# A gated mix of long convolution and multi-query attention on one core: x block 0 in two DMAs, the last x block by token chunks, the bound added to the first keys in place, and 88 instead of 92 score pairs on VectorE

## The chip, the core and the metric

The kernel runs on one core of a Trainium2 chip. The metric is the time of one execution on the device in microseconds (us). A profile of one execution belongs to it: the span is the time from the first to the last instruction in that profile. PE is TensorE, DVE is VectorE, ACT is ScalarE, POOL is GpSimd and SP is SyncE, which issues most DMAs.

## The reference: what is computed

S is 2048 tokens, D is 640 channels, there are 32 heads of 20 channels, and all heads share one key and one value of 20 channels. All inputs are bf16. Cut to what matters (left out: y is the causal convolution of kv with ssm_k along the tokens, by FFT):

```python
def _A_ref(q, k, v, shift_k, ssm_k, ssm_D):
    k_pad = jnp.pad(k, ((0, 0), (ks - 1, 0), (0, 0)))
    for t in range(ks):
        k_shift = k_shift + k_pad[:, t:t + S, :] * shift_k[:, ks - 1 - t][None, None, :]
    kv = k_shift * v
    ...
    y = y + kv * ssm_D[None, None, :]
    return q * y

def _B_ref(x, wq, wk, wv, wo):
    q = (x @ wq).reshape(B, S, H, Dh).transpose(0, 2, 1, 3)
    k = x @ wk
    v = x @ wv
    scores = jnp.einsum("bhqd,bkd->bhqk", q, k) * (Dh ** -0.5)
    p = _softmax(scores, axis=-1)
    o = jnp.einsum("bhqk,bkd->bhqd", p, v)
    return o.transpose(0, 2, 1, 3).reshape(B, S, H * Dh) @ wo

x = A_q
g = _sigmoid((x * gate_w).sum(-1, keepdims=True))
return g * _A_ref(x, A_k, A_v, A_shift_k, A_ssm_k, A_ssm_D) + (1 - g) * _B_ref(x, B_wq, B_wk, B_wv, B_wo)
```

## The kernel before

**A graph and a planner.** The kernel doesn't issue instructions as it goes. The methods of the class `Kernel` add operations (`Op`) to a graph: engine, function, keys read and written, an estimated cost and a priority. `Scheduler.run` (L204) then plays the program through once at build time with these costs, engine by engine, and picks for each engine the ready operation with the lowest priority number. The result is one fixed order for each engine, which `emit` (L544) writes out with the semaphore waits. On the chip every engine runs its order strictly; where the plan was off, an engine waits, and all that stands behind it in its order waits too. Where PE would be idle, the planner puts in filler matmuls: against zeros into an unused bank before attention starts (L1704), and against zeros into the accumulator (L1699) later. Matmul operations belong to groups that take one of 8 PSUM banks from a list and are evacuated by DVE or ACT.

**The work of attention.** Queries come in 4 blocks of 512 tokens; a head group is 4 heads on 4 x 32 rows of PE. So there are 32 (block, group) steps, named by G; a step has 16 key blocks j of 128 keys, and in each 4 score tiles (one per head r) of 128 keys x 512 queries. The last step (LASTG = 31) is split by queries into three stages (`STAGES`). `stream` (L1144) lines up all tiles in order and takes out those that go to DVE: for step G and each j in `DVE_J[G]` two of the four heads form a pair that DVE exponentiates by a polynomial (`DEXP`, L1231: two score matmuls, two L1257 out of PSUM, then L1260, L1261, L1263). It does this only where G < LASTG. The other tiles go to ACT in units of 3 and 2 by turns: `QK` (L1197, matmuls L1190) writes a unit's scores to PSUM banks 0 to 2 (ETA) or 3 to 4 (ETB), `EXP` (L1225, L1227) exponentiates them, and `PV` (L1273, L1268) multiplies the result with the values into a bank that gathers the step's output. The units of QK, EXP and PV are the main line; everything else is placed around it.

**Softmax without a maximum pass.** Each score gets a bound subtracted by way of the matmul itself: row 20 of each head's 32 query rows holds an estimate of the query's length (`cr`, from the squares of the queries: L1110, matmul L1118, L1124), and row 20 of the keys holds a factor from the largest key length (`mcol`, L1071). The row of the queries is written by a small DMA on SP (L1127, "qT<-cr"). So the scores of a group need its query projection (L1095), the square, the sum over a head's channels, `cr` and that DMA; and all scores need `mcol`.

**The prologue**, before the first exp:
- `loads` (L833): SP issues x block 0 (512 tokens x 640), the weights of the first query group, x blocks 1 to 3, then, when block 3 has landed, the rest of wq. ACT issues wk, wv and the gate's weights.
- `tables` (L892): the cosine and sine tables for the convolution, made by DVE (L905, L908) and ACT (L910).
- `weights`, `weights2`: POOL puts the weights into padded tiles; `wq_pad` is set to zero first (L869 for group 0, L991 for the rest), then filled (L984 and L995).
- `xT` (L999): PE transposes x by 128x128 blocks (L1008), ACT or DVE copies each bank of them to SBUF (L721, L720). Blocks 0 to 2 go in groups of two 128-channel slices, block 3 slice by slice.
- `kproj` (L1019): for each x block, L1035 makes keys, values and gate for each of its 4 token chunks (41 columns, "kvn"); ACT squares the keys (L1043), DVE sums (L1054) and takes the maximum (L1057), PE spreads it to all partitions (L1060), and three small DVE operations make `mcol` (L1064, L1068, L1071). The transposed keys come from L1027 per x block; the evacuation adds `mcol` per partition: the first 128 keys by ACT (L1081), all others by DVE (L1079).
- `qproj` (L1087): group 0 before the attention, then groups 1 and 2, 3 and 4, 5 and 6, 7 in its course (bank 7 alone), then the later query blocks (`qproj_next`).

**Around the attention** run the shifted keys of the convolution (`kshift`, L1467: DMA transposes and loads of v on SP, `kdiag` on DVE, L1494 on PE), the rest of the tables (`tables2`, L919), the convolution by matmuls with the tables (L1551, L1617; products on POOL, L1584) and the output projection (L1647). `norm` (L1332) divides a finished step. For the last step, `tail_o` (L1380) and `tail` (L1406) do so with short operations: transposes and a reciprocal on DVE (L1389, L1393, L1394, L1397), a last product (L1403) added to partial sums made ahead (`part`, L1364: L1373 and L1376), and L1458 for the last rows.

## Time and profile before

| | |
|---|---|
| runs of the kernel before | 872.35 us median of 3 (872.23 to 873.17) |
| the profiled execution | 872.47 us; its span 870.7 us |
| granted clock of TensorE | 0.999 |
| PE busy | 846.3 us (97%), 8157 matmuls |
| ACT busy | 856.9 us (98%), 769 instructions |
| DVE busy | 699.7 us (80%) |
| POOL busy | 380.4 us (44%) |
| L1227, ETA of 128x1536 | 373 times, 1628 ns mean |
| L1227, ETB of 128x1024 (and one of 128x512) | 373 times, 1205 ns mean |
| L1260, L1261, L1263 on DVE, 128x1024 | 92 times each, 1397, 1384 and 1446 ns mean |
| L1257 on DVE, 128x512 out of PSUM | 184 times, 687 ns mean |
| filler matmuls of L1699 | 944 |

A line of the profile's page or of its timeline names engine, line of the source, operation and what is written from what ("ETA<-ps"), with the count after an x. In a timeline the first number is the start in us from the span's start, the second the time in us that the instructions of the line cover; in brackets stands the idle time before and what ended it. In the chain of waits each piece is followed back from the last instruction to what released it. "SPq" is SP issuing a DMA; "issue" is time without a cause that the profile shows. A busy share is an average over the whole span: it doesn't tell which engine sets the end.

### The profile page before, as it was taken

Reading aid. Unit: us, or ns where it says so; the run is one execution under the profiler, and the core shown is the slowest. Engines: PE = TensorE matmul, PEld = TensorE weight load, DVE = VectorE, ACT = ScalarE, POOL = GpSimd, SP = SyncE. Lnnn points to the kernel's source line nnn. Section 1 sums busy time; section 2 is a strip of 40 time slices with the busy share of each in tenths; the row PEclk is TensorE's granted clock in tenths of the full one; section 3 lists DMA queues with packets and bytes.
Section 4 is the critical chain, followed back from the end, with each engine's and each line's share of the span. In section 5 each row is a group of like instructions: output and inputs, shape, how many; then the busy total and the mean of one; then the engine's idle time right before and its main releaser. Section 6 shows DMA issues by size and latency. Waiting matters only on the chain.

```text
span 870.7 us, 18888 instructions
## 1 busy us (share of the span) xinstructions
PE 846.3 (97%) x8157; PEld 352.7 (41%) x8177; DVE 699.7 (80%) x905; ACT 856.9 (98%) x769; POOL 380.4 (44%) x351
## 2 busy tenths in 40 slices
PE   8999999999999999999999999999999999999998
PEld 5334434443444344444334344444343344243344
DVE  8568884489899887988888888887889879888835
ACT  6999999999999999999999999999999999999997
POOL 4573005767434255635345745456761345710000
PEclk9999999999999999999999999999999999999999
DMA  6900020002000001000001120000100000040210
GB/s 196 209 15 8 22 44 14 14 14 43 20 21 15 16 12 44 20 21 14 20 8 32 33 58 14 20 11 17 45 20 20 14 11 4 14 112 29 66 67 33
DMA packets 49714, 30.72 MB, mean 35 GB/s; under 512 B 32477, under 2 KB 45662, under 8 KB 49630
## 3 DMA queue, kind: packets, MB, share of 16 engines
q1 hardware_dynamic: 49054, 29.29, 12.6%
q8 instruction: 64, 1.05, 0.5%
q10 hardware_dynamic: 576, 0.22, 0.1%
q14 instruction: 20, 0.16, 0.1%
HBM read 17.85 MB, written 6.02 MB: 27 GB/s over the span
## 4 chain that ended last, share of the span: by engine, by line
ACT 93%; PE 5%; DMA 1%; DVE 0%; SPq 0%; issue 0%
ACT ETA L1227 55%; ACT ETB L1227 38%; PE ps L1190 1%; DMA xn<-in_A_q_dram 1%; PE ps L1373 1%; PE ps L1095 1%; PE ps L1268 1%; PE ps L1494 1%; PE ps L1403 0%; PE ps L1008 0%; SPq L687 0%; PE ps L1035 0%; PE ps L1027 0%; PE ps L1118 0%; DVE outsb L1458 0%
## 5 line engine op out<-in xcount | busy, mean ns | idle before, releaser
L1227 ACT ACTIVATE ETA<-ps 128x1536 bf16<-128x1536 f32 x373 | 607.1, 1628 | 0.6 <-PE ps L1190 0.5
L1227 ACT ACTIVATE ETB<-ps 128x1024 bf16<-128x1024 f32 (+1 forms) x373 | 449.4, 1205 | 1.3 <-PE ps L1190 1.3
L1190 PE MATMUL ps<-qT,kT 32*128 32x512 bf16 (+2 forms) x2176 | 301.0, 372 | 14.5 <-ACT ETA L1227 8.0
L1584 POOL TENSOR_TENSOR Pp<-X,K 128x512 f32<-128x512 bf16 x120 | 164.0, 1383 | 146.5 <-DVE K L1572 48.9
L1257 DVE TENSOR_SCALAR dW<-ps 128x512 f32<-128x512 f32 x184 | 126.3, 687 | 65.9 <-PE ps L1190 64.4
L1190 PEld LDWEIGHTS ps<-qT,kT 32*128 32x128 bf16 x2176 | 76.5, 91 | 247.4 <-ACT ETB L1227 128.1
L1268 PE MATMUL ps<-ETA,vaug 128*32 128x512 bf16 (+2 forms) x1196 | 153.9, 371 | 0.0
L1268 PE MATMUL ps<-ETB,vaug 128*32 128x512 bf16 (+2 forms) x796 | 148.5, 371 | 0.0
L1263 DVE SCALAR_TENSOR_TENSOR ETd<-dX,dW 128x1024 int16<-128x1024 f32 x92 | 133.1, 1446 | 3.2 <-PE ps L1268 3.1
L1260 DVE SCALAR_TENSOR_TENSOR dX<-dW 128x1024 f32<-128x1024 uint16 x92 | 128.5, 1397 | 1.0
L1261 DVE SCALAR_TENSOR_TENSOR dX<-dX,dW 128x1024 f32<-128x1024 f32 x92 | 127.3, 1384 | 0.4
L1584 POOL TENSOR_TENSOR AB<-Pp 128x256 bf16<-128x256 f32 x80 | 66.1, 826 | 68.3 <-DVE dX L1260 24.6
L1617 PE MATMUL ps<-AB,Tcs 128*128 128x256 bf16 x600 | 89.4, 275 | 0.0
L1551 PE MATMUL ps<-ssm_kT,Tcs 128*128 128x256 bf16 x600 | 89.0, 275 | 0.0
L1551 PE MATMUL ps<-kv,Tcs 128*128 128x256 bf16 x600 | 87.4, 275 | 0.1
L1348 POOL TENSOR_TENSOR oTn<-acc,rbc 128x512 bf16<-128x512 f32 x24 | 39.9, 1661 | 88.5 <-DMA rbc<-scr_d 27.7
L1699 PE MATMUL ps<-Tcs,zeros 128*32 128x512 bf16 x944 | 77.9, 385 | 0.7 <-DVE acc L1336 0.5
L1584 POOL TENSOR_TENSOR Pp<-Pp 128x512 f32<-128x512 f32 x40 | 53.9, 1348 | 39.3 <-DVE dX L1261 19.1
L1617 PEld LDWEIGHTS ps<-AB,Tcs 128*128 128x128 bf16 x600 | 51.6, 97 | 34.3 <-issue 27.1
L1551 PEld LDWEIGHTS ps<-ssm_kT,Tcs 128*128 128x128 bf16 x600 | 50.6, 97 | 32.5 <-issue 25.9
L1551 PEld LDWEIGHTS ps<-kv,Tcs 128*128 128x128 bf16 x600 | 49.7, 97 | 34.2 <-issue 27.5
L1348 POOL TENSOR_TENSOR oT<-acc,rbc 128x512 bf16<-128x512 f32 x7 | 8.9, 1272 | 85.3 <-DMA rbc<-scr_d 60.3
(133 smaller groups left out, 650.8 us busy)
## 6 DMA issues: line engine op xcount, KB each, us to landing
rbc<-scr_d SPq DMA_DIRECT2D x31, 256.0 KB
scr_o<-oTn SPq DMA_DIRECT2D x24, 128.0 KB, 1.7
xn<-in_A_q_dram SPq DMA_DIRECT2D x4, 640.0 KB, 8.3
kv<-in_A_v_dram SPq DMA_DIRECT2D x4, 640.0 KB, 4.7
out_dram<-outsb SPq DMA_DIRECT2D x15, 160.0 KB, 1.8
oTp<-scr_o SPq DMA_DIRECT2D x12, 160.0 KB, 2.7
wog<-in_B_wo_dram SPq DMA_DIRECT2D x4, 200.0 KB
wo<-in_B_wo_dram SPq DMA_DIRECT2D x4, 200.0 KB, 3.2
```

The costliest lines, as they stand in the source:

```text
L1190: return e.matmul(self.bank(bk, n, n * t), T["kT4"][32 * r:32 * r + 32, 128 * jt:128 * jt + 128], T[k][32 * r:32 * r + 32, g, q0:q0 + n], ...
L1227: op("act", lambda e: e.activation(et(n)[:, 0:w], self.ps[:, lo:lo + w], ACT.Exp, scale=SCALE), [("ps", base[n % 2] + k) for k in range(le ...
L1257: self.evac(gr, "dve", lambda e, bk, h=h: e.tensor_scalar(W[:, 512 * h:512 * h + 512], self.bank(bk), SCALE * LOG2E * 128.0, 128.0 * (127 ...
L1260: V(lambda e: e.scalar_tensor_tensor(X[:, :], w, DP, w, ALU.add, ALU.mult), [kW], ["dX"], c_ps(1024), **k)
L1261: V(lambda e: e.scalar_tensor_tensor(X[:, :], X[:, :], DQ, w, ALU.add, ALU.mult), [kW], ["dX"], c_ps(1024), **k)
L1263: V(lambda e: e.scalar_tensor_tensor(T[f"ETd{pe}"][:, :].bitcast(dt.int16), X[:, :], DA, W[:, :], ALU.mult, ALU.add), [kW, "dX"], [("ETd", ...
L1268: return op("pe", lambda e: e.matmul(self.bank(b, n)[32 * r:32 * r + 32, :], T[va][:, j, :], src, start=(j == 0), stop=(j == NSC - 1), til ...
L1348: self.pool(lambda e: e.tensor_tensor(out, T["acc"][:, :], T["rbc"][:, :], ALU.mult), ["acc", "rbc"], [key], c_pool(512), prio=p, port=Tru ...
L1551: self.mm(gr, lambda e, bk, lhs=lhs, rhs=rhs, comp=comp, n=n: e.matmul(self.bank(bk, 256, 256 * comp), lhs, rhs, start=(n == 0), stop=(n = ...
L1584: f = lambda e: e.tensor_tensor(out, a, b, alu)
L1617: self.mm(gr, lambda e, bk, lhs=lhs, fc=fc, comp=comp, h=h: e.matmul(self.bank(bk, 256, 256 * h), lhs, AB[:, fc, :, comp, :], start=(fc == ...
L1699: sch.filler, *sch.filler2 = ([[lambda e, r=r, st=st, b=b, n=n: e.matmul(self.bank(b, n)[32 * r:32 * r + 32, :], self.T["zeros"][:, 0:32], ...
```

## The change

The change has these parts; lines in the text are those of the kernel before.

1. `loads`: x block 0 is loaded by two DMAs of two token chunks each, with a key for each half.
2. `xT`: block 0 is transposed by halves (4 slices in a bank, then 1), blocks 1 and 2 as before, block 3 by token chunks (one bank holds all 5 slices of 128 tokens). `xkeys` names the pieces that a reader needs (L1035, L1027 and L1095 read by it).
3. `kproj`: the first key slab of 512 is split in 128 and 384, each a group of its own. The first 128 keys are copied out of PSUM by DVE without `mcol`, before `mcol` is known, and `mcol` is added to them in SBUF by a DVE operation of its own (`kTm`). The other 384 are evacuated by ACT with `mcol` added. The later slabs wait for the copy of the first instead of the maximum's matmul.
4. `weights2`: the zeroing of `wq_pad` for groups 1 to 7 is cut in 5 parts, which come after the square of query group 0; keys are per group, so a group's projection waits for its own weights alone.
5. `qproj`: groups 1 to 7 of the first block may use banks 7 and 5; their squares get an early priority for groups 1 and 2. `vneg` comes after the last key slab.
6. `DVE_J` is another list: 88 entries, none in the last row. The old one has 94, two of them in the row of step 31.
7. Estimated costs of some matmuls in the planner (0.068 to 0.0565 for a transpose, 0.034 to 0.0265 for kvn).

Since the planner runs again with all this, the order of all engines differs from the first instructions to the last, the placing of fillers too.

```diff
@@ -632,7 +632,7 @@
 LASTG = 31
-DVE_J = [(), (), (9,), (5,), (6,), (1, 4, 8, 12), (1, 10, 13), (1, 5, 9, 13), (2, 9, 11), (2, 7, 12), (3, 8, 13), (3, 6, 13), (2, 7, 12), (1, 4, 8, 12), (1, 5, 10, 12), (3, 9, 12), (1, 4, 8, 12), (1, 7, 12), (4, 11), (1, 5, 9, 13), (3, 8, 13), (1, 4, 8, 12), (2, 9, 12), (1, 5, 11), (2, 6, 10, 14), (2, 5, 10, 13), (3, 8, 11), (2, 10), (2, 3, 8, 11, 14), (1, 4, 7, 10, 14), (1, 6, 11), (3, 9)]
+DVE_J = [(), (6,), (), (5, 12), (1, 5, 9, 13), (3, 11), (5, 12), (3, 8, 13), (3, 8, 13), (1, 6, 11), (3, 8, 13), (3, 8, 13), (3, 8, 13), (1, 5, 9, 13), (2, 9), (4, 9, 14), (1, 6, 11), (2, 7, 12), (2, 7, 12), (3, 8, 13), (2, 6, 10, 14), (2, 7, 12), (3, 8, 13), (1, 6, 11), (3, 8, 13), (3, 8, 13), (3, 11), (3, 6, 9, 12), (2, 5, 8, 11, 14), (2, 5, 8, 11, 14), (4, 9, 14), ()]
@@ -835,8 +835,10 @@
         x = aps["A_q"][0].rearrange("(i p) d -> p i d", p=128)
         wq = aps["B_wq"].rearrange("(p dc) n -> p dc n", dc=NDC)
         for b in range(NB):
-            xl = self.dma(T["xn"][:, 4 * b:4 * b + 4, :], x[:, 4 * b:4 * b + 4, :], writes=[("xn", b)], nbytes=440000,
-                          prio=-9 + b, lat=6.0)
+            for lo, hi in ((0, 2), (2, 4)) if b == 0 else ((0, 4),):
+                xl = self.dma(T["xn"][:, 4 * b + lo:4 * b + hi, :], x[:, 4 * b + lo:4 * b + hi, :],
+                              writes=[("xn", b) if b else ("xnh", lo)], nbytes=110000 * (hi - lo),
+                              prio=-9 + b + 0.1 * lo, lat=6.0)
             if b == 0:
                 self.dma(T["wqst"][:, :, 0:80], wq[:, :, 0:80], writes=[("wqst", 0)], prio=-8.5, lat=5.0)
         self.xl = [xl]
@@ -988,30 +990,38 @@
         dst = T["wq_pad"][:, :, :].rearrange("p k (h c) -> p k h c", c=32)
         src = T["wqst"][:, :, :].rearrange("p k (h c) -> p k h c", c=20)
-        self.pool(lambda e: e.memset(T["wq_pad"][:, :, 128:1024].bitcast(I32), 0), (), [("wq_pad", 1)], 2.0, prio=-8.9,
-                  after=[self.g.writer["wk4"]])
+        for k in range(NDC):
+            self.pool(lambda e, k=k: e.memset(T["wq_pad"][:, k, 128:1024].bitcast(I32), 0), (), [("wq_pad", g) for g in range(1, 8)], 0.45,
+                      prio=-8.9, after=[self.g.writer["sq", 0]])
         self.wq_cp = []
         for lo, hi in ((4, 8), (8, 16), (16, 24), (24, 32)):
             self.wq_cp.append(self.pool(lambda e, lo=lo, hi=hi: e.tensor_copy(dst[:, :, lo:hi, 0:20], src[:, :, lo:hi, :]),
-                      [("wqst", 1)], [("wq_pad", 1)], 0.75 if hi - lo == 4 else 1.5, prio=-4, name="wq_cp",
+                      [("wqst", 1)], [("wq_pad", g) for g in range(lo // 4, hi // 4)], 0.75 if hi - lo == 4 else 1.5, prio=-4 + 0.01 * lo, name="wq_cp",
                       after=self.crow0 + [self.g.writer["kT4", NB - 1, 0]]))
     def xT(self):
-        for b, d0, nd in ((b, d0, min(w, NDC - d0)) for b in range(NB) for w in (1 + (b < NB - 1),)
-                         for d0 in range(0, NDC, w)):
+        plan = [(0, c0, 2, d0, nd) for c0 in (0, 2) for d0, nd in ((0, 4), (4, 1))]
+        plan += [(b, 0, 4, d0, min(2, NDC - d0)) for b in range(1, NB - 1) for d0 in range(0, NDC, 2)]
+        plan += [(NB - 1, c, 1, 0, NDC) for c in range(4)]
+        for b, c0, nc, d0, nd in plan:
             gr = self.group("xT", 0.5 + 0.1 * b, banks=(0, 1, 2, 3, 4, 5, 7))
+            n = 128 * nc
             for dc in range(d0, d0 + nd):
-                for ci in range(4):
-                    i = 4 * b + ci
-                    self.mm(gr, lambda e, bk, i=i, dc=dc, ci=ci, d0=d0: e.transpose(
-                        self.bank_bf(bk, 128, 512 * (dc - d0) + 128 * ci), T["xn"][:, i, dc:D:NDC],
-                        T["ident"][:, :]), [("xn", b), "ident"], 0.068)
-            out = T["xT"][:, d0:d0 + nd, 512 * b:512 * b + 512]
-            al = self.copy_alts(out, lambda bk, nd=nd: self.bank_bf(bk, 512 * nd).rearrange(
+                for ci in range(nc):
+                    i = 4 * b + c0 + ci
+                    self.mm(gr, lambda e, bk, i=i, dc=dc, ci=ci, d0=d0, n=n: e.transpose(
+                        self.bank_bf(bk, 128, n * (dc - d0) + 128 * ci), T["xn"][:, i, dc:D:NDC],
+                        T["ident"][:, :]), [("xn", b) if b else ("xnh", c0), "ident"], 0.0565)
+            out = T["xT"][:, d0:d0 + nd, 512 * b + 128 * c0:512 * b + 128 * c0 + n]
+            al = self.copy_alts(out, lambda bk, nd=nd, n=n: self.bank_bf(bk, n * nd).rearrange(
                 "p (d t) -> p d t", d=nd), True)
-            self.evac(gr, "dve", None, (), [("xT", b, dc) for dc in range(d0, d0 + nd)], 0.45, alts=al)
+            self.evac(gr, "dve", None, (), [("xT", b, dc, c0) for dc in range(d0, d0 + nd)], 0.45, alts=al)
+    def xkeys(self, b, dc, ci=None):
+        w = 2 if b == 0 else 1 if b == NB - 1 else 4
+        return [("xT", b, dc, c0) for c0 in range(0, 4, w) if ci is None or c0 <= ci < c0 + w]
     def kkey(self, j):
         return "kT4", j // 4, 128 if 0 < j < 4 else 0
@@ -1020,13 +1030,14 @@
-        for b in range(NB):
-            gr = self.group("kT", (1.9 if b == 0 else 4.0) + 0.1 * b, banks=(5, 7))
+        slabs = [(0, 0, 128), (0, 128, 512)] + [(b, 0, 512) for b in range(1, NB)]
+        for n, (b, lo, hi) in enumerate(slabs):
+            gr = self.group("kT", (1.9 if n == 0 else 4.0) + 0.1 * n, banks=(5, 7))
             self.kTg.append(gr)
             for dc in range(NDC):
-                self.mm(gr, lambda e, bk, b=b, dc=dc: e.matmul(
-                    self.bank(bk), T["wk4"][:, dc, :], T["xT"][:, dc, 512 * b:512 * b + 512], start=(dc == 0),
-                    stop=(dc == NDC - 1)), [("xT", b, dc), "wk4"], c_mm(512))
+                self.mm(gr, lambda e, bk, b=b, dc=dc, lo=lo, hi=hi: e.matmul(
+                    self.bank(bk, hi - lo), T["wk4"][:, dc, :], T["xT"][:, dc, 512 * b + lo:512 * b + hi], start=(dc == 0),
+                    stop=(dc == NDC - 1)), self.xkeys(b, dc) + ["wk4"], c_mm(hi - lo))
         for b in range(NB):
             gr = self.group("kvn", 0.65 + 0.1 * b, banks=ALLB)
             for ci in range(4):
...
@@ -1070,19 +1081,23 @@
             ["kmaxr"], ["kroot"], 0.2, prio=-5000, name="kmax")
         self.dve(lambda e: e.tensor_scalar(T["mcol"][:, :], T["kroot"][:, :].bitcast(F32), T["m20"][:, 0:1],
                                            T["q21"][:, 0:1], ALU.mult, ALU.add), ["kroot", "m20", "q21"], ["mcol"], 0.2, prio=-5000, name="kmax")
-        for b in range(NB):
-            gr = self.kTg[b]
-            for lo, hi in ((0, 128), (128, 512)) if b == 0 else ((0, 512),):
-                n = hi - lo
-                out = T["kT4"][:, 512 * b + lo:512 * b + hi]
-                alts = {
-                    "dve": ((lambda e, bk, out=out, lo=lo, n=n: e.tensor_scalar(
-                        out, self.bank(bk, n, lo), T["mcol"][:, 0:1], None, ALU.add)), c_ps(n)),
-                    "act": ((lambda e, bk, out=out, lo=lo, n=n: e.activation(
-                        out, self.bank(bk, n, lo), ACT.Identity, bias=T["mcol"][:, :])), c_act(n))}
-                mine = "act" if b == 0 and lo == 0 else "dve"
-                alts = {mine: alts[mine]}
-                self.evac(gr, mine, None, ["mcol"], [("kT4", b, lo)], 0.7, alts=alts)
+        for m, (b, lo, hi) in enumerate(slabs):
+            gr, n = self.kTg[m], hi - lo
+            out = T["kT4"][:, 512 * b + lo:512 * b + hi]
+            key = ("kT4", b, lo)
+            if m == 0:
+                self.evac(gr, "dve", lambda e, bk, out=out: e.tensor_copy(out, self.bank(bk, 128)), (), [key], c_ps(n),
+                          prio=-4000.0)
+                self.dve(lambda e, out=out: e.tensor_scalar(out, out, T["mcol"][:, 0:1], None, ALU.add), ["mcol"], [key],
+                         0.2, prio=-5000, port=True, name="kTm")
+                for x in self.kTg[2:]:
+                    x.mms[0].deps.add(self.g.writer[key])
+            elif m == 1:
+                self.evac(gr, "act", lambda e, bk, out=out, n=n: e.activation(
+                    out, self.bank(bk, n), ACT.Identity, bias=T["mcol"][:, :]), ["mcol"], [key], c_act(n))
+            else:
+                self.evac(gr, "dve", lambda e, bk, out=out, n=n: e.tensor_scalar(
+                    out, self.bank(bk, n), T["mcol"][:, 0:1], None, ALU.add), ["mcol"], [key], c_ps(n))
     def qproj(self, I, gs, prio, banks, ng):
@@ -1095,7 +1110,7 @@
                 o = self.mm(gr, lambda e, bk, gi=gi, dc=dc: e.matmul(
                     self.bank(bk), T["wq_pad"][:, dc, 128 * gi:128 * gi + 128],
                     T["xT"][:, dc, 512 * I:512 * I + 512], start=(dc == 0), stop=(dc == NDC - 1)),
-                    [("wq_pad", 0 if gi < 1 else 1), ("xT", I, dc)], c_mm(512))
+                    [("wq_pad", gi)] + self.xkeys(I, dc), c_mm(512))
                 if dc == 0:
                     o.deps.update(self.crow0 or ())
@@ -1109,7 +1124,7 @@
                                                                        bias=T["qup"][:, :])), c_act(512))})
             self.dve(lambda e, gi=gi, gl=gl: e.tensor_tensor(T[f"sq{gl}"][:, :], qt[:, gi, :], qt[:, gi, :],
                                                              ALU.mult),
-                     [(f"qT{par}", gi)], [("sq", gl)], c_fast(512), prio=-1500.0 if I == 0 and gs[0] == 0 else prio - 500, port=True,
+                     [(f"qT{par}", gi)], [("sq", gl)], c_fast(512), prio=-1500.0 if I == 0 and gs[0] < 3 else prio - 500, port=True,
                      name="sq")
         gr = self.group("q2", prio - 500, banks=banks)
         ind = T[f"IndG{ng}"]
@@ -1167,7 +1182,7 @@
         self.pool(lambda e: e.tensor_scalar(T["vneg"][:, :, :], T["vaug"][:, :, :], -(2.0 ** KDN), 1.0, ALU.mult,
                                             ALU.mult), ["vaug"] + [("vaugb", b) for b in range(NB)], ["vneg"],
-                  c_pool(512), prio=14.0, name="vneg", after=self.crow0)
+                  c_pool(512), prio=14.0, name="vneg", after=self.crow0 + [self.g.writer["kT4", NB - 1, 0]])
@@ -1676,7 +1691,7 @@
         self.kproj()
         for b, gs in enumerate(([0], [1, 2], [3, 4], [5, 6], [7])):
-            self.qproj(0, gs, 0.61 if b == 0 else 3.0 + 6 * b, ALLB if b == 0 else (7,), 2)
+            self.qproj(0, gs, 0.61 if b == 0 else 3.0 + 6 * b, ALLB if b == 0 else (7, 5), 2)
             if b == 0:
                 self.weights2()
```

More of the change, by code (lines that the diff above doesn't have):

```diff
@@ L1036, in kproj @@
                         self.bank(bk, 41, 44 * ci), T["xT"][:, dc, 128 * tc:128 * tc + 128], T["wkv"][:, dc, 0:41],
-                        start=(dc == 0), stop=(dc == NDC - 1)), [("xT", b, dc), "wk", "wv", "wg"], 0.034)
+                        start=(dc == 0), stop=(dc == NDC - 1)), self.xkeys(b, dc, ci) + ["wk", "wv", "wg"], 0.0265)
             def view(bk, lo, n=20):
```

## The prediction

> **What bounds the kernel now.** I read the page's chain of work that ended last first, then the timeline of ACT, then the chain of the first 23 us, then the windows around ACT's gaps and around the end.
>
> ```profile
> ACT 93%; PE 5%; DMA 1%; DVE 0%; SPq 0%; issue 0%
> ```
>
> ACT carries the end for 93% of the span; PE is busy 97% but carries 5%. ACT's timeline shows how full it is (start, duration):
>
> ```profile
> 20.67 1.45 ACT L1227 ACTIVATE ETA<-ps 128x1536 bf16<-128x1536 f32 x1 [0.54 <-PE ps L1190]
> ...
> 51.54 1.45 ACT L1227 ACTIVATE ETA<-ps 128x1536 bf16<-128x1536 f32 x1
> 52.87 1.03 ACT L1227 ACTIVATE ETB<-ps 128x1024 bf16<-128x1024 f32 x1
> 53.77 1.47 ACT L1227 ACTIVATE ETA<-ps 128x1536 bf16<-128x1536 f32 x1
> ...
> 863.00 1.63 ACT L1227 ACTIVATE ETA<-ps 128x1536 bf16<-128x1536 f32 x1
> 864.35 0.77 ACT L1227 ACTIVATE ETB<-ps 128x512 bf16<-128x512 f32 x1
> ```
>
> The starts run ahead of the work, so durations grow (1.45, 1.47, later 1.7); the ends keep the true pace. ETA ends: 51.54+1.45 = 52.99, then 53.77+1.47 = 55.24. Over all pairs the end-to-end distance is 2.26 us (1.343 for an ETA of three score tiles, 0.917 for an ETB of two, so 0.426 per tile of 512 columns and 0.065 per instruction). From the first ETA's end (22.12) to the last one's (864.63) are 372 pairs: 372 x 2.26 = 840.72 of 842.51 us. All stalls of ACT in 844 us are therefore 1.79 us, and one of them is 1.36:
>
> ```profile
> 47.64 0.60 SPq L687 DMA_DIRECT2D qT<-cr  x1
> 47.65 1.72 ACT L1227 ACTIVATE ETA<-ps 128x1536 bf16<-128x1536 f32 x1
> ...
> 50.16 0.60 PE L1190 MATMUL ps<-qT,kT 32*128 32x512 bf16 x5
> 50.62 1.02 ACT L1227 ACTIVATE ETB<-ps 128x1024 bf16<-128x1024 f32 x1 [1.26 <-PE ps L1190]
> ```
>
> 50.62 is the 26th exp instruction, the first that holds a tile of head group 1 (64 tiles in group 0, five per pair). Its scores read row 20 of that group's queries, which the DMA issued at 47.64 brings (1.8 us for the first such: issued 15.60, SP goes on at 17.39). So PE could not score before about 49.4, and its fixed order had put ten L1494, five L1095 and seven L1494 in the hole.
>
> So the time is: start of the first exp + exp work + stalls + tail. What sets the start:
>
> ```profile
> 2.65 8.31 DMA xn<-in_A_q_dram
> 10.96 0.05 issue
> 11.00 1.09 PE ps L1008 x16
> 12.09 0.05 issue
> 12.14 1.03 PE ps L1095 x4
> ...
> 14.48 0.38 PE ps L1118
> 14.86 1.25 PE ps L1008 x20
> ```
>
> PE waits for x block 2 and transposes it before the first query projection L1095; L1118 then waits for DVE's square; only then come block 3's transposes (that block had landed by 12.68, when SP issues the load behind it).
>
> **What the Trainium skill says.** "Perfetto Trace Analysis", section "DVE / Act Engine Instruction (TENSOR_ADD, Activation, etc)": the reported end is when the write is acknowledged and the semaphore pushed. The trace agrees: ends are evenly spaced by 2.26 us where starts are not, so I count ends. "SBUF — State Buffer", section "Who interferes with whom": a DVE instruction in a two-port mode and a GpSimd instruction lock each other out of a shared pair for a whole instruction. The trace agrees:
>
> ```profile
> 7.63 2.12 POOL L991 MEMSET wq_pad<- 128x2240 int32 x1
> 7.87 2.15 DVE L908 TENSOR_SCALAR tprod<-tprod 128x514 int32<-128x514 int32 x1
> ```
>
> The 514 column L908 takes 2.15 us beside the memset, while one of 770 columns took 0.55. "DMA: Bandwidth & Descriptors", section "Anatomy of one DMA": about 2 us fixed per DMA, most of it completion; here 1.8 for the 4 KB row DMA, and I use 1.8.
>
> **The change, part by part.**
>
> *Pairs, 92 to 88.* The old table has 94 entries, but its last row (two) belongs to group 31, which `stream` does not give to DVE, and the page counts 92 of L1260. Four fewer pairs are eight more tiles for ACT. The built programs have 373 ETA, 372 ETB and one ETB of one tile before; 374, 374 and one ETA of two tiles after. That is +1.343 +2 x 0.917 +0.917 -0.491 = **+3.60 us**, all on the bound. What it saves on DVE (4 x (2 x 0.69 +1.40 +1.38 +1.45) = 22 us) and what PE gains by other placing shortens no exp; it can only remove stalls.
>
> *Group 1's stall.* The change lets group 1 and 2's projection use two banks, gives each group its own key for the padded weights, and puts the table transposes later. In the changed order on PE both squares' sums (L1133) stand beside exp unit 18 instead of 23, the row DMA follows them, and the first matmul that waits for it (the scores of the pair at group 1, key block 6) stands behind unit 22's scores, unit 25's main scores three units later. Unit 18's scores run at about 20.1 + 8.5 x 2.26 = 39.3; sums 0.4, cr 0.67, DMA 1.8: landed at about 42.5. PE comes to the waiting matmul at 20.1 + 10.5 x 2.26 = 43.8 and ACT would starve only near 46. The SP queue ahead of it (four transposes of about 4.15 and four kv loads of 0.58 from 17.7) is through at about 37. So **-1.36**, with 1 to 3 us of cover; if the cover is gone, the stall is back. The small stalls (1.79 - 1.36 = 0.43) I leave as they are, 0 to 0.8.
>
> *The start.* Block 0 in two DMAs costs SP one more issue (0.56, the median) ahead of the first weights and blocks 1 to 3. Either the queue is fed from what waits in it (0) or each later block shifts by a whole issue (0.56); I take 0.3. Block 1 landed at 9.2 (1.98 + the shortest landing 7.2), now 9.5. PE reaches it at 8.36 less three filler matmuls (0.64) plus 20 transposes (1.25) plus a filler (0.2) = 9.2, so it starts at 9.5. The new PE order from there: transposes of block 1 (1.25), projection (1.03), kvn (0.50), block 2 (1.25), L1133 (0.38), kvn (0.50), block 3 (1.25), kvn (0.50), two fillers (0.44), kvn (0.50): 7.6, so the last kvn ends at 17.1 where it ended at 17.54: -0.44. Block 3 (12.97) and block 2 (11.3) are in before PE asks (14.4 and 12.3). Between kvn and L1060's matmul the five L1027 of 512 columns (1.02) and a filler become five of 128 columns (0.3) and four fillers (0.85): the same 1.15. DVE is the second clock here: evacuations, square (13.3), cr, two chunk copies of 0.46 and sums fill it from 11 to 18, so any of them late by 0.1 delays the last kvn or the maximum as much.
>
> *The bound in place.* Before: from mcol (ends 19.72) ACT's kT (0.37) to the scores at 20.18, 0.46. Now DVE adds it in SBUF: not in the trace; between 0.15 (L881) and 0.27 (L866, 128x128), I take 0.22, with handovers 0.30: -0.16. The other 384 columns go through ACT (0.37 + 256 x 0.832 ns = 0.58) while DVE and PE prepare the scores (0.03 + 0.22 + 0.05 + 0.49 = 0.79): covered by 0.2; without that cover it costs 0.2. Start together: **-0.60** (0 to -1.1), first exp at 20.07.
>
> *At no cost.* The memset of 2.12 now runs in five parts of about 0.43 behind the square (13.3 to 15.5). It holds DVE's L910 no more, and DVE's work there comes out of PSUM, as the cr and xT copies beside POOL's casts at 14.98 and 15.93, which show no stretch. Behind it on POOL stand the vaug copies (14.98 before), which PE needs at 24.9. vneg behind the wq copies and kv behind the first transpose have users after 40 us. Each has over 5 us.
>
> *Tail.* The last L1376 (865.24, on DVE ahead of the last transpose) moves forward:
>
> ```profile
> 865.24 0.55 DVE L1376 SCALAR_TENSOR_TENSOR part<-ps,omgf,kv 128x320 f32<-128x320 f32 x1 [0.26 <-PE ps L1373]
> ...
> 865.71 0.31 DVE L1389 STREAM_TRANSPOSE acc<-ps 128x128 f32<-128x128 f32 x1
> ```
>
> The scores' last product ends at 865.58, so the transpose gains **-0.08**; the rest of the 5.55 us stays.
>
> Sum: 870.67 + 3.60 - 1.36 - 0.60 - 0.08 = 872.23 span. The profiled execution took 872.47, 1.8 over its span, and lies 0.12 over the median: **873.9**, 0.18% over 872.35.
>
> **The rivals.**
>
> *A stall takes the place of the one removed (slower).* Place: the first two groups, where kdiag, four projections, the table transposes and the new DVE pair of group 1 share DVE and PE. If the row DMA lands after about 46, ACT waits again. Against it: cr would have to be 3 us late. For it: ACT's old stalls lie in the first 200 us. It decides from 0.2 us on; at the old size, 873.9 + 1.36 = 875.3. Chance 0.18.
>
> *The start gains nothing (slower).* Blocks shift by a whole issue and DVE is late by 0.3: 874.5. For it: 7.2 to 9.5 us to landing shows full queues. Chance 0.08.
>
> *The start gains twice as much.* Block 1 is not later (0.3) and kvn needs no fillers (0.44), small stalls gone: 872.9 to 873.2. Chance 0.12.
>
> *The freed engines make it faster.* Even with every stall (1.79) gone and 1.5 at the start: 872.35 + 3.60 - 1.79 - 1.5 - 0.08 = 872.6. A gain over 0.2% needs cheaper exps, for which nothing speaks. Chance 0.04.
>
> **The numbers.** The forecast's case has 0.58, its own range 873.2 to 874.6. A measurement of this kernel can tell about 0.2%, 1.74 us, from no change: slower begins at 874.1, faster ends at 870.6. Of the 0.58, 0.40 lie within and 0.18 above. Within: 0.40 + 0.12 = 0.52; slower: 0.18 + 0.18 + 0.08 = 0.44; faster 0.04. The range reaches over the rivals on both sides: 872.9 to 875.4.
>
> **What would show it.** Right: 374 ETA and 374 ETB of unchanged pace (2.26); first exp at 19.6 to 20.6; no gap of over 0.3 near the 26th exp; last exp's end to the span's end near 5.5. Wrong: another pace of the ends; a gap of about 1 us before 110 us; block 1's transposes later than 9.8; a first exp before 19.4.

## The result, and the profile after

| | before | after |
|---|---|---|
| median of 22 runs each, us | 872.37 (871.92 to 873.22) | 873.9 (873.42 to 874.7) |
| ratio after / before, 95% interval | | 1.0017 (1.0011 to 1.0024) |
| profiled execution, us; its span | 872.47; 870.7 | 873.42; 871.6 |
| exps on ACT; pairs on DVE | 746; 92 | 749; 88 |
| first exp starts, last exp ends | 20.67, 865.12 | 19.77, 866.16 |
| stalls of ACT between exp ends (beyond 1.343, 0.917 and 0.491 us for 3, 2 and 1 tiles) | 1.79 | 0.12 |
| last exp's end to the span's end | 5.55 | 5.46 |
| DVE busy; POOL busy | 699.7; 380.4 | 675.9; 375.2 |

The changed kernel is 1.5 us (0.17%) slower. From here on lines are those of the changed kernel; they lie 2 to 15 above the old ones (L1227 is now L1242, L1190 is L1205, L1373 is L1388, L1376 is L1391). The page's chain of waits, after:

```profile
ACT 97%; PE 1%; DMA 1%; DVE 0%; SPq 0%; issue 0%
```

ACT's share rose from 93 to 97%: more exps and fewer holes. ACT's timeline after, at the start, where the 26th exp stalled before (that place is now 48 to 53), and at the end:

```profile
19.77 1.45 ACT L1242 ACTIVATE ETA<-ps 128x1536 bf16<-128x1536 f32 x1 [0.17 <-PE ps L1205]
...
48.25 1.02 ACT L1242 ACTIVATE ETB<-ps 128x1024 bf16<-128x1024 f32 x1
49.15 1.46 ACT L1242 ACTIVATE ETA<-ps 128x1536 bf16<-128x1536 f32 x1
50.48 1.04 ACT L1242 ACTIVATE ETB<-ps 128x1024 bf16<-128x1024 f32 x1
...
864.04 1.20 ACT L1242 ACTIVATE ETB<-ps 128x1024 bf16<-128x1024 f32 x1
864.94 1.21 ACT L1242 ACTIVATE ETA<-ps 128x1024 bf16<-128x1024 f32 x1
```

Ends are 49.27, 50.61, 51.52: again 1.34 and 0.91, with no bracket for a wait. The pace is the old 2.26 us per ETA and ETB; 374 full ETA, one of 1024 columns (the last line) and 374 ETB are 3.60 us more work. SP's and PE's timeline in group 1:

```profile
41.71 0.60 SPq L687 DMA_DIRECT2D qT<-cr  x1
...
44.04 0.40 PE L1205 MATMUL ps<-qT,kT 32*128 32x512 bf16 x4
```

The row DMA is issued 5.9 us earlier than before (47.64), and at 44.04 the scores that need it run without a wait in brackets. The chain of the first 20 us after (start, duration, what):

```profile
2.50 6.74 DMA xn<-in_A_q_dram 
9.24 0.05 issue
9.29 1.31 PE ps L1014 x20
...
15.37 0.50 PE ps L1046 x20
15.87 0.44 PE ps L1719 x2
16.31 0.50 PE ps L1046 x20
16.81 0.28 PE ps L1038 x5
17.09 0.86 PE ps L1719 x4
17.95 0.17 PE ps L1071
```

The chain now comes from x block 1 (landed at 9.24) where it came from block 2. Two groups of fillers (L1719) stand in it, 1.3 us; what they cost is tried below (refit_less_fill). And the collision of memset and table work is gone:

```profile
9.26 0.42 DVE L910 TENSOR_SCALAR tprod<-tprod 128x514 int32<-128x514 int32 x1
...
12.98 2.59 POOL L994 MEMSET wq_pad<- 128x448 int32 x5 [5.40 <-DVE sq L1125]
```

The instruction on 514 columns that took 2.15 us beside the memset takes 0.42 without it.

The sum of the two profiles: +3.60 exps, -0.90 start, -1.67 stalls, -0.09 tail, +0.94; the spans differ by 0.95. So the four pairs given up cost more than start and stall gave back. The open question was what they bought: why not keep 92 pairs and take the 2.57 us? In the changed profile the side work (everything on PE and DVE that is not exps or their products) is through early. Its last piece is the partial output sums, `part`. DVE's instructions for them after, with first and last start:

```profile
L1391 DVE SCALAR_TENSOR_TENSOR part<-ps,omgf,kv x8: 509/551/552, 843.8 to 857.1; 128x320 f32<-128x320 f32 x8
```

and before:

```profile
L1376 DVE SCALAR_TENSOR_TENSOR part<-ps,omgf,kv x8: 550/551/551, 848.7 to 865.2; 128x320 f32<-128x320 f32 x8
```

Before, the last of these stood at 865.2, with the end of the last exp: two chains ended together there, ACT's and that of the side work. After, it starts 9 us ahead of the last exp's end.

### The profile page after: what moved, and what is told of

It is laid out like the page before. It is cut to its first block, busy times and chain, and to the rows that moved or that the text cites. A ratio compares the mean times of both kernels' runs of the same rounds, so it can differ in the third digit from the quotient of the medians.

```text
span 871.6 us, 18985 instructions
## 1 busy us (share of the span) xinstructions
PE 848.0 (97%) x8220; PEld 351.0 (40%) x8239; DVE 675.9 (78%) x888; ACT 859.3 (99%) x770; POOL 375.2 (43%) x355
## 4 chain that ended last, share of the span: by engine, by line
ACT 97%; PE 1%; DMA 1%; DVE 0%; SPq 0%; issue 0%
ACT ETA L1242 58%; ACT ETB L1242 39%; DMA xn<-in_A_q_dram 1%; PE ps L1014 0%; PE ps L1046 0%; SPq L687 0%; PE ps L1719 0%; PE ps L1110 0%; DVE outsb L1473 0%; PE ps L1205 0%; PE ps L1418 0%; PE ps L1283 0%; DVE acc L1404 0%; DVE oT L1412 0%; PE ps L1133 0%
## 5 line engine op out<-in xcount | busy, mean ns | idle before, releaser
L1242 ACT ACTIVATE ETA<-ps 128x1536 bf16<-128x1536 f32 x375 | 607.5, 1620 | 0.2 <-PE ps L1205 0.2
L1242 ACT ACTIVATE ETB<-ps 128x1024 bf16<-128x1024 f32 x374 | 448.7, 1200 | 0.0
L1205 PE MATMUL ps<-qT,kT 32*128 32x512 bf16 (+2 forms) x2176 | 299.8, 371 | 12.1 <-ACT ETA L1242 5.0
L1599 POOL TENSOR_TENSOR Pp<-X,K 128x512 f32<-128x512 bf16 x120 | 157.2, 1326 | 186.9 <-DVE K L1587 73.3
L1205 PEld LDWEIGHTS ps<-qT,kT 32*128 32x128 bf16 x2176 | 75.7, 91 | 241.2 <-ACT ETB L1242 124.7
L1272 DVE TENSOR_SCALAR dW<-ps 128x512 f32<-128x512 f32 x176 | 120.9, 688 | 47.0 <-PE ps L1205 45.7
L1283 PE MATMUL ps<-ETB,vaug 128*32 128x512 bf16 (+2 forms) x798 | 150.6, 371 | 0.9 <-ACT ETA L1242 0.9
L1278 DVE SCALAR_TENSOR_TENSOR ETd<-dX,dW 128x1024 int16<-128x1024 f32 x88 | 121.7, 1383 | 23.4 <-PE ps L1283 23.2
L1276 DVE SCALAR_TENSOR_TENSOR dX<-dX,dW 128x1024 f32<-128x1024 f32 x88 | 123.3, 1401 | 0.6
L1275 DVE SCALAR_TENSOR_TENSOR dX<-dW 128x1024 f32<-128x1024 uint16 x88 | 122.7, 1394 | 1.2
L1599 POOL TENSOR_TENSOR AB<-Pp 128x256 bf16<-128x256 f32 x80 | 62.9, 787 | 54.4 <-DVE dX L1275 19.9
L1714 PE MATMUL ps<-Tcs,zeros 128*32 128x512 bf16 (+1 forms) x1000 | 79.7, 378 | 2.0 <-DVE acc L1351 1.5
L1599 POOL TENSOR_TENSOR Pp<-Pp 128x512 f32<-128x512 f32 x40 | 56.2, 1406 | 32.0 <-DVE ETd L1278 13.9
L1566 PEld LDWEIGHTS ps<-kv,Tcs 128*128 128x128 bf16 x600 | 49.4, 98 | 36.1 <-issue 28.4
```

The lines of the kernel that those rows point to most:

```text
L1205: return e.matmul(self.bank(bk, n, n * t), T["kT4"][32 * r:32 * r + 32, 128 * jt:128 * jt + 128], T[k][32 * r:32 * r + 32, g, q0:q0 + n], ...
L1242: op("act", lambda e: e.activation(et(n)[:, 0:w], self.ps[:, lo:lo + w], ACT.Exp, scale=SCALE), [("ps", base[n % 2] + k) for k in range(le ...
L1272: self.evac(gr, "dve", lambda e, bk, h=h: e.tensor_scalar(W[:, 512 * h:512 * h + 512], self.bank(bk), SCALE * LOG2E * 128.0, 128.0 * (127 ...
L1275: V(lambda e: e.scalar_tensor_tensor(X[:, :], w, DP, w, ALU.add, ALU.mult), [kW], ["dX"], c_ps(1024), **k)
L1276: V(lambda e: e.scalar_tensor_tensor(X[:, :], X[:, :], DQ, w, ALU.add, ALU.mult), [kW], ["dX"], c_ps(1024), **k)
L1278: V(lambda e: e.scalar_tensor_tensor(T[f"ETd{pe}"][:, :].bitcast(dt.int16), X[:, :], DA, W[:, :], ALU.mult, ALU.add), [kW, "dX"], [("ETd", ...
```

## The experiments

Each table row below is one kernel's profile; "part" is the start of its last DVE instruction for `part`, "tail" goes from the last exp's end to the span's end.

| kernel | pairs | median us | first exp | stalls | last exp ends | part | tail |
|---|---|---|---|---|---|---|---|
| before | 92 | 872.37 | 20.67 | 1.79 | 865.12 | 865.2 | 5.55 |
| after | 88 | 873.9 | 19.77 | 0.12 | 866.16 | 857.1 | 5.46 |
| old_list | 92 | 882.19 | 20.43 | 1.04 | 864.14 | 875.3 | 16.6 |
| fewer_pairs | 88 | 878.95 | 21.40 | 3.68 | 871.34 | 870.6 | 6.3 |
| only_group1 | 92 | 880.36 | 19.68 | 0.69 | 863.03 | 872.5 | 14.9 |
| only_start | 92 | 884.72 | 21.09 | 6.56 | 870.31 | 877.5 | 12.6 |
| refit_after | 95 | 871.74 | 19.95 | 2.49 | 862.35 | 864.3 | 7.33 |
| refit_before | 94 | 873.29 | 21.29 | 3.65 | 865.77 | 864.3 | 5.47 |
| refit_less_fill | 95 | 871.27 | 20.45 | 1.98 | 862.34 | 864.3 | 7.32 |
| refit_lead | 95 | 870.92 | 19.54 | 2.09 | 861.54 | 863.5 | 7.33 |
| one_dma | 88 | 876.26 | 20.98 | 1.93 | 869.18 | 866.2 | 5.49 |
| one_dma_lead | 88 | 875.97 | 20.01 | 2.43 | 868.70 | 865.7 | 5.47 |
| one_key | 88 | 878.51 | 21.00 | 3.98 | 871.25 | 868.2 | 5.47 |
| bank7 | 88 | 876.29 | 20.01 | 1.14 | 867.41 | 869.1 | 7.08 |

### The parts by themselves

**old_list**: the changed kernel with the table of pairs of before.

```diff
-DVE_J = [(), (6,), (), (5, 12), ...]
+DVE_J = [(), (), (9,), (5,), ...]
```

> The changed kernel with the old list of pairs (92 carried out). Theory (the exp stream of ACT is the bound, so the time is first exp + exps + stalls + tail): 8 tiles fewer on ACT than in the changed kernel, so 3.6 us less: 373 ETA, 372 ETB and one ETB of one tile, first exp at 19.6 to 20.0, stalls up to 0.5, time near 870.3. Rival (the 88 pairs were needed, because with 92 DVE or PE falls behind and ACT waits): the 3.6 us come back as gaps of ACT of 1.5 us or more, time 872 or above.

Measured: 882.19 us (4 runs), ratio 1.0109 (1.0093 to 1.0124). The exps did end 2.0 us earlier than after, and the program 9.1 us later. The chain of old_list from the last exps on:

```profile
864.90 2.47 PE ps L1388 x18
867.37 0.03 issue
867.39 0.56 DVE part L1391
867.95 0.05 issue
868.00 0.45 PE ps L1418 x2
868.44 0.01 issue
868.46 1.82 PE ps L1388 x12
```

ACT is done at 864.14; PE still has 48 products of `part` (L1388) ahead, and between them go DVE's sums and the last products (L1418), until 877.5. My forecast had costed this chain at nothing. With the old list in the new prologue it is the bound by 11 us.

**fewer_pairs**: the kernel before, with four pairs less (in steps 14, 16, 21 and 24), nothing else.

```diff
-(1, 5, 10, 12) ... (1, 4, 8, 12) ... (1, 4, 8, 12) ... (2, 6, 10, 14)
+(1, 5, 10) ... (1, 6, 11) ... (2, 7, 12) ... (3, 8, 13)
```

> The kernel before with one pair less in each of the steps 14, 16, 21 and 24 (88 carried out), nothing else changed. Theory: plus 8 tiles, +3.6 us, first exp and the 1.36 us gap at the 26th exp as before, time near 876.0. Rival (a lighter DVE lets ACT run with fewer waits): less than +2.5 us.

Measured: 878.95 us (5 runs), ratio 1.0072 (1.0059 to 1.0084): 6.6 us slower for 3.6 us of exps. Of the span's +6.9 us, 1.9 are new stalls (1.08 of them at 510), 0.7 a later first exp in the same prologue, 0.7 the tail. So 88 pairs don't by themselves end the side work early: `part` is at 870.6 here and at 857.1 in the changed kernel. The rule "fewer pairs, earlier side work" fails. The later first exp need not be the edit's: the chain of the start runs over the 18 leading fillers here, and they, the same as before, took 7.00 us in this profile and 5.71 in that of before.

**only_group1**: before with the group's own key for the weights, the memset in parts, two banks, early squares and late `vneg`; list and start of before. **only_start**: before with the DMAs, transposes, keys and estimated costs of the change alone.

```diff
 only_group1
-                    [("wq_pad", 0 if gi < 1 else 1), ("xT", I, dc)], c_mm(512))
+                    [("wq_pad", gi), ("xT", I, dc)], c_mm(512))
```

> The kernel before with the parts for head groups 1 to 7 alone (weights zeroed in 5 parts after the first square, a key for each group's weights, banks 7 and 5, early squares for groups 1 and 2, vneg later). Theory: the gap at the 26th exp goes, -1.4 us, the first exp stays at 20.7 within 0.3: time near 870.9. Rival (the gap goes because the keys come otherwise, not by these parts): a gap of over 0.8 us remains and the time is above 871.8.

> The kernel before with the parts for x and the keys alone (block 0 in two DMAs, block 3 by chunks, first keys in place), its list of pairs and its group weights as before. Theory: first exp 0.9 us earlier, at 19.8, and the gap at the 26th exp stays at about 1.4 or grows by what the start gains, because the row DMA of group 1 comes no earlier: time 871.4 to 872.4. Rival (the start is worth its full 0.9 us alone and the gap doesn't grow): 871.4 or less.

Measured: 880.36 (ratio 1.009, 1.0077 to 1.0104) and 884.72 us (1.0145, 1.0131 to 1.0159), 9.5 and 13 us over what I expected. only_group1 has no gap at the 26th exp; the row DMA is issued at 38.57. Its first exp was expected to stay at 20.7 within 0.3; it stands at 19.68, 0.99 earlier than before, without any of the parts for x and the keys. Its chain at the start:

```profile
10.41 1.08 PE ps L1096 x5
...
11.99 0.91 PE ps L1009 x16
...
19.68 1.45 ACT ETA L1228
```

The first projection (L1096) comes ahead of block 2's transposes (L1009) here, as in the changed kernel; before, it stood behind them and behind the wait for that block, at 12.14. The leading fillers ended 0.34 earlier in this profile (8.18 against 8.52), which may be a part of it. In only_start the gap grows to 4.9 us:

```profile
48.11 1.55 ACT L1241 ACTIVATE ETA<-ps 128x1536 bf16<-128x1536 f32 x1
54.45 1.02 ACT L1241 ACTIVATE ETB<-ps 128x1024 bf16<-128x1024 f32 x1 [4.79 <-PE ps L1204]
```

The theory for this gap, an earlier start with the row at its old time, doesn't fit: the start came later, and the row DMA is issued at 51.69, 4 us later than before. Both kernels end with a tail of side work (`part` at 872.5 and 877.5). Judged by total time, the parts for group 1 alone look like a loss of 8 us, though their own terms are gains: the gap is gone, and the last exp ends at 863.03, 2.1 us earlier than before. The total says only that the list no longer fits the order. only_start starts late (first exp at 21.09, 1.08 of it a wait of ACT for the first scores): the maximum's matmul is 0.49 us earlier than before (18.35 against 18.84), but PE's order has two projection matmuls ahead of the first scores, and they wait for ACT's copy of the keys until 20.06. So the parts of the start alone didn't bring the first exp forward, and those for group 1 alone did: what the first exp gained in the changed kernel can't be put down to the x halves, the chunks and the bound in place.

### Is it the number of pairs or where they stand?

**refit_after**: the changed prologue with a table looked for anew, 95 pairs. **refit_before**: the same search for the prologue of before, 94 pairs.

```diff
 refit_after
+DVE_J = [(), (11,), (4, 12), (4, 9, 13), (2, 4, 8, 9, 13), (6, 8, 13), (6, 13), (8, 10), (3, 10), (2, 10, 12), (5, 7, 10, 14), (4, 10), (8, 14), (2, 7, 11, 12), (3, 5, 11, 13), (2, 7, 11), (4, 10), (2, 6, 8, 13, 14), (3, 6, 9, 12), (4, 6, 12), (10,), (2, 8, 12), (1, 4, 8, 9, 14), (1, 7, 9, 14), (6, 9, 10, 14), (3, 6, 8), (4, 10), (3, 6, 8, 11, 13), (3, 8, 9), (3, 7, 11, 14), (2, 3, 9, 11, 14), ()]
```

> The changed kernel with another list of pairs, 95 instead of 88, looked for anew for its prologue. Theory (where the pairs stand decides whether the side work on TensorE and VectorE is through before the last exps, not how many there are): seven pairs more on VectorE take 14 tiles off ScalarE at 0.45 us, 6.3 us; some tenths come back as stalls; 873.9 - 6.3 + 0.7 = 868.3 us, 867.8 to 869.8, with the last output partial (L1388) done by about 866. Rival (VectorE's time alone holds the side work: in the runs with 92 pairs it ended 8 us later than with 88): seven pairs at some 4.2 us of VectorE end it 14 us later than 856.7, at about 871, and the kernel takes 877 us or more.

> The kernel before with its list looked for anew in the same way, 94 pairs instead of 92. Theory: two pairs more take 4 tiles off ScalarE, 1.8 us, less some tenths of stalls: 870.6 us, 870.2 to 871.6; the changed kernel with its new list is then faster by about the 2.5 us that its start and the stall of group 1 are worth (0.90 + 1.67). Rival (the new prologue is worth nothing and all is the list): both with new lists within 0.7 us of each other. Rival of VectorE's time: two pairs more end the side work 4 us later, 875.

Measured: refit_after 871.74 us (13 runs), ratio to before 0.9991 (0.9982 to 0.9999); refit_before 873.29 us (13 runs), 1.0006 (0.9997 to 1.0014), no better than before and 2.7 us over what I expected. With 95 pairs `part` stands at 864.3, 11 us earlier than with 92 in old_list on the same prologue: the place of the pairs decides, as the theory said. What in their place does it (which engine then waits for what) was not followed up. And the theory's number missed by 3.4 us; the rival's, 877 or more, was further off. The exps lost 6.3 us as expected; 2.4 came back as stalls (0.25 to 0.45 us each, at 300 to 485 and 800 us) and 1.9 in the tail. DVE's timeline of refit_after at the end:

```profile
862.66 0.54 DVE L1442 SCALAR_TENSOR_TENSOR outsb<-ps,omgf,part 128x320 bf16<-128x320 f32 x1
863.12 0.31 DVE L1404 STREAM_TRANSPOSE acc<-ps 128x128 f32<-128x128 f32 x1
863.35 0.51 DVE L1442 SCALAR_TENSOR_TENSOR outsb<-ps,omgf,part 128x320 bf16<-128x320 f32 x1
863.78 0.16 DVE L1408 RECIPROCAL rcp<-acc 128x4 f32<-128x4 f32 x1
864.28 0.55 DVE L1391 SCALAR_TENSOR_TENSOR part<-ps,omgf,kv 128x320 f32<-128x320 f32 x1 [0.34 <-PE ps L1388]
864.75 0.28 DVE L1409 TENSOR_TENSOR oTn<-acc,rcp 128x128 bf16<-128x128 f32 x1
```

The last step's normalization (L1404, L1408, L1409) has the last partial sum in its midst. The side work ends the program again, with a tail 1.9 us longer than after: both chains count, and the list balances them. The rival was half right too: DVE's time does count. From 88 to 95 pairs, both placed to suit the prologue, `part` moved by 7.2 us.

What is the prologue worth when each side has its own list? 873.29 to 871.74, 1.55 us, where I expected 2.5; the profile of refit_before holds 3.65 us of stalls and a first exp at 21.29, so its list may not be its best. I call 1.55 a size, not a bound.

### The start

**one_dma**: the changed kernel with x block 0 in one DMA.

```diff
-            for lo, hi in ((0, 2), (2, 4)) if b == 0 else ((0, 4),):
+            for lo, hi in ((0, 4),):
```

> The changed kernel with x block 0 in one DMA again (its transposes stay in four groups). Theory (TensorE is busy with its leading matmuls until 7.6 us, while both halves had landed by 5.4, so the splitting is hidden): block 0's transposes start within 0.1 us of the end of the leading matmuls, as in the changed kernel, and the first exp stands at 19.5 to 20.5. Rival (the halves' earlier landing carries the start): transposes wait for the DMA, by 0.3 us or more, first exp at 20.3 or later. The end depends on the order of the side work, which moves with every edit: 873.5 to 876.

Measured: 876.26 us (3 runs), ratio 1.004 (1.0026 to 1.0055), first exp at 20.98. The transposes follow the fillers at once, so PE didn't wait for the DMA; but the planner, which expects the whole block later, had put in 18 leading fillers instead of 15, and they lasted until 9.24. That neither theory had named: the first exp is late (by 1.2 us, out of the expected range) through fillers in the fixed order, not through the transfer. The rest of the 3.0 us by which the span grew, 1.8, are new stalls of ACT, 1.0 of them at 859, in an order that was planned anew. **one_dma_lead** takes nine of them out after planning.

```diff
+        fills = [o for o in sch.order["pe"] if o.name == "fill"]
+        drop = set(fills[9:18])
+        sch.order["pe"] = [o for o in sch.order["pe"] if o not in drop]
```

> The changed kernel with x block 0 in one DMA, and 9 of its 18 leading matmuls left out, so that TensorE asks for the block at 6.3 to 6.6 us. Theory (the split is hidden: the block lands whole by 6.6, and block 1 half a microsecond earlier than 9.24 since one issue of SP is saved): no wait for block 0 of over 0.2 us, block 1's transposes at 8.8 to 9.3, first exp at 19.3 to 20.0. Rival (the halves land earlier, and carry the start): TensorE waits for the block until 7 us or later, and block 1's transposes start after 9.5.

Measured (one run): 875.97 us. PE's timeline:

```profile
2.70 4.02 PE L1718 MATMUL ps<-ident,zeros 128*128 128x512 bf16 x9 [2.70 <-DVE ident L867]
6.52 2.33 PE L1013 MATMUL ps<-ident,xn 128*128 128x128 bf16 x20
9.19 1.31 PE L1013 MATMUL ps<-ident,xn 128*128 128x128 bf16 x20 [0.34 <-DMA xn<-in_A_q_dram]
```

The whole block was there when the fillers ended, at 6.6. In the changed kernel PE first asks for it at 7.43, so there the split of the DMA carries nothing on the chip. Block 1 landed at 9.14, against 9.24 with the extra issue in front, though it was issued 0.5 earlier. That difference says little: in the profiles that show it, block 1 landed at 8.42 to 9.16 with one DMA for block 0 and at 8.19 to 9.47 with two. The first exp, at 20.01, is 0.24 later than after; 2.33 us for block 0's transposes are twice what they take elsewhere.

**refit_less_fill** and **refit_lead**: refit_after without some of PE's fillers.

```diff
 refit_less_fill
+        drop = set(fills[len(fills) - 6:])
 refit_lead
+        drop = set(fills[9:15] + fills[len(fills) - 6:])
```

> The kernel with 95 pairs, and the last 6 of the 15 matmuls that only keep TensorE busy before x block 0 left out. In some executions these took 5.6 us instead of 4.9 and put the first exp at 20.43 instead of 19.77. Theory (the leading matmuls, cold at 0.43 us each, hold the start in part of the executions): first exp at 19.6 to 19.9 whatever the number of cold ones, median 0.1 to 0.5 us below that of the kernel with 95 pairs, spread of its runs smaller. Rival (TensorE's clock is not up without them): the transposes of block 0 run cold, first exp after 20.2, 0.3 to 1 us slower.

The edit took out other fillers than this says: not six of the 15 leading ones, but the six that stand at 15.9 and 17.1 in the chain above. So it says nothing on the theory. It was 871.27 us (21 runs; ratio to before 0.9985, 0.9978 to 0.9991), 0.47 less than refit_after, though the intervals of the two ratios overlap. Its profile shows what the leading ones do:

```profile
2.70 5.88 PE L1719 MATMUL ps<-ident,zeros 128*128 128x512 bf16 x15 [2.70 <-DVE ident L868]
8.42 1.28 PE L1014 MATMUL ps<-ident,xn 128*128 128x128 bf16 x20
...
10.23 0.95 PE L1014 MATMUL ps<-ident,xn 128*128 128x128 bf16 x14 [0.32 <-ACT xT L721]
```

The same 15 matmuls take 5.88 us here and 4.89 in the profile of after, and block 1 is taken up at 10.23; the bracket names ACT's copy of block 0, not the DMA. From there to the first exp (20.45) it took 10.22 us, against 10.49 in refit_after: the six fillers are 1.3 us of the chain, but without them only 0.27 is gained, as DVE's copy of the keys and its sums then stand in the chain instead.

> The kernel with 95 pairs without twelve of TensorE's matmuls that only keep it busy: the six of 15.9 to 18.0 us that were left out before, and the last 6 of the 15 that lead the program. Those 15 took 4.9 to 5.9 us in the profiles, as more or fewer of them ran at 0.43 us instead of 0.21. Theory (the leading ones hold the start where they are slow): nine end by 6.6 us even if all run cold, x block 0 is transposed before block 1 lands at 9.24, block 1's transposes start at 9.3 to 9.5 in every execution, first exp at 19.3 to 19.7; median 0.2 to 0.7 us below 871.27. Rival (TensorE is cold without them): block 0's and block 1's transposes take 2.5 us instead of 1.3, first exp after 20.5, as slow or slower than 871.27.

Measured: 870.92 us (14 runs), ratio to before 0.9980 (0.9972 to 0.9988), the fastest kernel of this study, 1.5 us under before and 3.0 under after. PE's timeline:

```profile
2.81 3.80 PE L1719 MATMUL ps<-ident,zeros 128*128 128x512 bf16 x9 [2.81 <-DVE ident L868]
6.44 1.28 PE L1014 MATMUL ps<-ident,xn 128*128 128x128 bf16 x20
...
8.95 1.31 PE L1014 MATMUL ps<-ident,xn 128*128 128x128 bf16 x20 [1.01 <-DMA xn<-in_A_q_dram]
```

PE waits 1.0 us for block 1, which landed at 8.90, and the transposes before it are not slow (1.28 us). The first exp is at 19.54. The gain over refit_less_fill, 0.35 us, is of the size expected, but the intervals of the two ratios overlap, and the spread of the runs did not shrink (1.4 us in both), so the number of slow leading matmuls is not most of that spread.

### What removed group 1's stall

**one_key**: the changed kernel with one key for all padded weights. **bank7**: the changed kernel with bank 7 alone for groups 1 to 7.

```diff
 one_key
-                    [("wq_pad", gi)] + self.xkeys(I, dc), c_mm(512))
+                    [("wq_pad", 0 if gi < 1 else 1)] + self.xkeys(I, dc), c_mm(512))
 bank7
-            self.qproj(0, gs, ..., ALLB if b == 0 else (7, 5), 2)
+            self.qproj(0, gs, ..., ALLB if b == 0 else (7,), 2)
```

> The changed kernel with one key for all the padded weights, so that each group's projection waits for all four copies on GpSimd, in their order, and not for its own alone; two banks and late table transposes stay. If the key is what removed group 1's stall: a gap of 1 us or more comes back near the 26th exp (50 to 55 us). Rival (the second bank or the later table transposes removed it): no gap over 0.3 us there. The end moves with the order of the side work and says nothing here: 874 to 881.

> The changed kernel with bank 7 alone for the projections of groups 1 to 7, as before. If the second bank is what removed group 1's stall: a gap of 1 us or more near the 26th exp. Rival (the own key did): none over 0.3 us there, first exp and group 1's row DMA as in the changed kernel (issued at 41.7). The end moves with the side work: 873 to 877.

Measured (one run each): one_key 878.51 us, bank7 876.29 us. ACT of one_key:

```profile
48.03 1.54 ACT L1242 ACTIVATE ETA<-ps 128x1536 bf16<-128x1536 f32 x1
52.13 1.02 ACT L1242 ACTIVATE ETB<-ps 128x1024 bf16<-128x1024 f32 x1 [2.56 <-PE ps L1205]
```

With one key the gap is back, at twice its old size, and the row DMA is issued at 49.89. In bank7 no wait of ACT shows up to 80 us, and the DMA is issued at 44.43, 2.7 us later than with two banks. So without the group's own key the stall is back, and without the second bank it is not (one run each): the key is needed, and the bank only adds cover. With the key, group 1's projection needs the first of POOL's four copies (L998, which start at 28.4 to 33.5) and not the last. How much of the 8.2 us by which the row comes later in one_key is a wait for the copies (they end at 35.8) and how much the order that the planner then chose is not split: the next projection on PE starts at 40.33, and the second set of table transposes (L937) moved from 38.9 to 31.0, so "late table transposes" did not stay as the expectation has it. The late `vneg` and the early squares were not tried alone.

## Why the prediction was right, step by step

- **Pairs, +3.60**: exact in count and pace. "All on the bound" held too.
- **Group 1's stall, -1.36**: right, with less cover than worked out: cr came at 41.00 and the issue at 41.71, so with 1.8 us the row landed near 43.5 (an estimate; about 42.5 was expected), and PE came to the waiting matmul at 44.04 instead of 43.8. Of the three causes that I listed, the own key is shown to be needed and the bank not; the later table transposes were not tried alone.
- **Small stalls, "I leave as they are"**: mis-sized; 0.43 became 0.12, so all stalls gave 1.67.
- **The start, -0.60**: mis-sized, -0.90. The path is the one worked out, and its pieces were: block 1 landed at 9.24, not 9.5, which is luck in part, as that landing lies anywhere from 8.2 to 9.5 in the profiles, and SP's extra issue can't be priced from it. From block 1's transposes to the last kvn 7.6 were worked out and 7.52 taken. From there to the maximum's matmul I wrote "the same 1.15"; before it was 1.30 (17.54 to 18.84), after 1.14. The matmul itself and what follows to `mcol` were 0.10 longer. The bound in place gave 0.11 instead of 0.16: kTm took 0.26, not 0.22, and two table transposes (L937) held PE until 19.28. The 384 columns on ACT ended 0.17 ahead of the first exp, where 0.2 of cover was worked out. That these parts make the gain is not shown: only_group1, with none of them, has its first exp at 19.68, and only_start, with them alone, at 21.09.
- **The memset at no cost**: right; POOL zeroes from 12.98, and the trace shows no wait for it. Moving it may even be part of the start's gain, as it is among the parts of only_group1; it was not tried alone.
- **Tail, -0.08**: right, -0.09.

With the measured terms the span of the profiled execution is 871.6, 0.6 under the 872.23 of the forecast. That execution is the fastest of its 22, 0.48 under the median, while the one of before lies 0.10 over its own. So that the median meets the forecast to the digit is partly luck: terms too small by 0.6 and a profile lower than its median by about as much. The leading fillers, which took 4.8 to 5.9 us in profiles of the same 15, can make part of that distance; with one profile of the changed kernel this stays open.

Of the rivals, none took over. "The start gains twice" had half of its grounds: block 1 was not later and the small stalls went, but kvn kept its fillers.

One sentence of the forecast was wrong without hurting it: that what the fewer pairs save on DVE and PE "shortens no exp; it can only remove stalls". What leaves DVE and PE, or comes to them, also moves a second chain, which I had not looked for in the profile since it ended together with the last exp; where the pairs stand counts there for more than how many there are. The forecast escaped because the changed list fits its order, with `part` 9 us ahead; I walked into it in the experiments, where four kernels with an unfitted list missed by 3 to 13 us.

## What to carry to other kernels

When two chains end together, the profile's chain of waits shows one of them; look where the last piece of the other stands before costing at nothing what a part takes from it or gives it. Where a table is fitted to one order of the work, a part of a change can't be judged by total time with the old table: read its own term (first exp, the gap, the row's DMA), or fit the table again on both sides. And a step that came out as worked out on the changed kernel's trace is not yet put down to the part that it was worked out for: try that part alone and look at the same step. And fillers in a fixed order are work: once their cover is longer than the transfer they wait for, they hold the start.

## What the runs showed of the hardware that was not expected

The same leading matmuls (128x512, no inputs to wait for) took different times in different executions at a granted clock of 0.998 to 1.0: 15 of them 4.84, 4.89, 4.92, 4.96, 5.35, 5.62 and 5.88 us, 18 of them 5.48, 5.71, 6.54, 6.89 and 7.00 us. From start to start a matmul took about 0.43 us at first and 0.22 later, and what differed was the point at which it changed, after some 3.0 to 6.2 us of work. After nine of them and no gap, 20 transposes took 2.33 us in one kernel and 1.28 in another.
